# Regrouping a block's small matmuls, naming the PSUM banks they borrow, and moving two sums to GpSimd

## The chip, the core and the metric

One core of a Trainium2 chip runs the whole kernel. The metric is device microseconds (us) of one execution. TensorE multiplies and writes to PSUM, of which this kernel's pools hold eight banks. In this kernel VectorE and ScalarE read PSUM, and GpSimd works from SBUF. Most executions of one kernel here agree within about 1 us of 276, so differences under 0.5% are read from the traces. There the blocks in the middle of the kernel repeat to about 0.02 us, except block 5 of the kernel before: 14.85 us in its own trace, 14.75 and 14.77 in two runs that leave that block's code alone (light, tail).

## The reference, cut to what matters

```python
def reference(q, k, v, w_in, w_out, beta):        # 8 batches, 8 heads, 576 tokens, 64 per head
    # attention inside chunks of 64 tokens
    scores = (q_c @ k_c.T) / 8
    attn = softmax(scores)
    x = (attn @ v_c).transpose(0, 2, 1, 3).reshape(4608, 512)
    # feed-forward, d_ff = 2048
    h = x @ w_in
    g = h * sigmoid(beta * h)
    return g @ w_out
```

## The kernel before

It works through nine blocks, 0 to 8, of 512 tokens. From block 2 on, each block has a first GEMM (x @ w_in, then Silu on ScalarE) and a second (g @ w_out). The second, and one half of the first, save a product by sums and differences of quarters (seven products in place of eight). Beside them run the attention of the next block (PV: probabilities times v) and the scores of the one after that. PV works on 64x64 tiles of TensorE, the scores on 32x64 tiles, the GEMMs on the whole array.

The second GEMM is seven products of 16 matmuls, `mm[0]` to `mm[6]`, on banks A, B, A, D, A, C, A. A collects three sums in turn, which ScalarE copies out on the way (u1, u2, u3). Before the change banks come from a ring of four:

```python
ps_p = ctx.enter_context(tc.tile_pool(name="ps_p", bufs=4, space=bass.MemoryType.PSUM))
def grab(name):
    bank[name] = ps_p.tile([128, 2, HM], FP32, tag="p", name=f"o{name}")
def mm2():
    prod("A", s_(3), t3, False)
    take("u2", "A")                       # ScalarE copies A
    ...
    nc.gpsimd.tensor_tensor(out=sb["w1"], in0=sb["u1"], in1=sb["u2"], op=ALU.subtract)
def cB():                                 # VectorE adds u1 straight from bank B
    store(j, 0, 0, comb("B", sb["u1"]))
```

This is the order within a block, with lines joined and block 1's own calls left out (`late` is block 1, `light` are blocks 6 to 8, of which 8 has no PV left; `dve(n)` issues n waiting sums of quarters on VectorE; each `pvs` is two PVs and their normalisation):

```python
mm[0]()
if not late and not light: dve(2)
emit_sum(j, 3, 1); emit_sum(j, 3, 3)
...
pvs(0)
mm[1]()
if light: dve(2); pvs(2)
dve(6)
mm[2]()
if not late and not light: pvs(2)
if na + 1 < NB and not late: table(ACTF.Exp)
mm[3]()
for p in (0, 2, 1, 3): emit_sum(j, 4, p)  # s4, which mm[5] needs
cB()
mm[4]()
cD()
if na + 1 < NB:
    emit_sc(2 * na + 2, "x")              # 128 small matmuls in one run
    emit_sc(2 * na + 3)
T(j + 3); emit_xs(na)
mm[5](); cC(); mm[6]()
```

The softmax here doesn't subtract the row's maximum and nothing guards it: scores larger than these inputs give would overflow.

Of the kernel before, what the change touches and what calls it, by code (L numbers as in the profile page):

```python
# [8 lines left out]
FP32 = mybir.dt.float32  # L9
FP16 = mybir.dt.float16  # L10
# [5 lines left out]
def kernel(  # L16
# [10 lines left out]
    nc = tc.nc  # L27
# [27 lines left out]
    xs_p = ctx.enter_context(tc.tile_pool(name="xs", bufs=1))  # L55
    c_p = ctx.enter_context(tc.tile_pool(name="c", bufs=2))
    osb_p = ctx.enter_context(tc.tile_pool(name="osb", bufs=4))
    ps_p = ctx.enter_context(tc.tile_pool(name="ps_p", bufs=4, space=bass.MemoryType.PSUM))
    ps_s = ctx.enter_context(tc.tile_pool(name="ps_s", bufs=1, space=bass.MemoryType.PSUM))
    ps_x = ctx.enter_context(tc.tile_pool(name="ps_x", bufs=1, space=bass.MemoryType.PSUM))  # L60

    ident = const.tile([128, 128], FP16)
    bstage = const.tile([128, 2, 32], FP32)
# [84 lines left out]
    def sc_part(g, z, sc):  # L148
        for c in range(4):
            b, cb = divmod(4 * g + c, NCB)  # L150
            for e in range(2):
                for a in range(4):
# [8 lines left out]
                        stop=(e == 1),  # L161
                    )

    def emit_sc(g, where="s"):
        if where == "x":
            scx = ps_x.tile([128, 2, 2, 4, CH], FP32, tag="x", name="scx")
            sc = [scx[:, 0], scx[:, 1]]
        else:
            sc = [
                ps_p.tile([128, 2, 4, CH], FP32, tag="p", name=f"scp{s}") if where == "p"  # L170
                else ps_s.tile([128, 2, 4, CH], FP32, tag=f"sc{s}", name=f"sc{s}")
                for s in range(2)
            ]
        for z in range(2):
            sc_part(g, z, sc)
        et = et_t[g] = et_p.tile([128, 2, 2, 4, CH], FP16, tag="et", name="et")
        for o, i_ in [(et, scx)] if where == "x" else [(et[:, s], sc[s]) for s in range(2)]:
            nc.scalar.activation(out=o, in_=i_, func=ACTF.Exp, scale=scale)
# [16 lines left out]
        return x16.rearrange("p e s d -> p (e s d)")  # L195

    def emit_pv(i, where="x", xbar=True):
        g = i // 2
        spare = where != "x"
        if where == "p":  # L200
            xs = [ps_p.tile([128, 4, 128], FP32, tag="p", name="xp") for _ in range(2)]
        elif where == "s":
            xs = [ps_s.tile([128, 4, 128], FP32, tag=f"sc{h}", name="xp") for h in range(2)]
        else:
            x = ps_x.tile([128, 2, 4, 128], FP32, tag="x", name="x")
            xs = [x[:, 0], x[:, 1]]
        for s in range(4):
            z, a2 = s // 2, s % 2
            for hp, cp in ((0, 0), (1, 1), (0, 1), (1, 0)):
                b, cb = divmod(2 * i + cp, NCB)  # L210
                p0, o0 = 64 * hp, 64 * cp
                nc.tensor.matmul(  # L212
                    out=xs[hp][o0:o0 + 64, s, 0:D + 1],
                    lhsT=et_t[g][p0:p0 + 64, a2, z, 2 * (i % 2) + cp, :],
                    rhs=vbuf[b % NV][p0:p0 + 64, s, cb, 0:D + 1],
                )
        xf = normed(xs, None if spare else x)
        j, t0 = i // 4, (i % 4) * 128
        if j not in xt_t:
            xt_t[j] = xt_p.tile([128, KDM, BLK], FP16, tag="xt", name="xt")  # L220
        if xbar:
            nc.sync.dma_start_transpose(out=xt_t[j][:, :, t0:t0 + 128], in_=xf)
        else:
            x16_t[i] = xf

    def emit_xp(i, where="s", eng=None):
        xf = x16_t.pop(i)
        j, t0 = i // 4, (i % 4) * 128
        pool, tag = {"s": (ps_s, f"sc{i % 2}"), "p": (ps_p, "p"), "x": (ps_x, "x")}[where]
        xps = pool.tile([128, KDM, 128], FP16, tag=tag, name="xps")  # L230
        for kk in range(KDM):
            nc.tensor.transpose(
                out=xps[:, kk, :], in_=xf[:, kk * 128:(kk + 1) * 128], identity=ident
            )
        if eng:
            eng.tensor_copy(out=xt_t[j][:, :, t0:t0 + 128], in_=xps)
        else:
            nc.scalar.copy(out=xt_t[j][:, :, t0:t0 + 128], in_=xps)

    def emit_idle(n, w=512, d=None):  # L240
        if d is None:
            d = ps_p.tile([128, BLK], FP32, tag="p", name="idle")
        for _ in range(n):
            nc.tensor.matmul(
                out=d[:, 0:w], lhsT=zero[:, 0:128], rhs=zero[:, 0:w], start=True, stop=True)
        return d
# [6 lines left out]

    def emit_h(j, m, c0=0, c1=BLK, ns=range(KDM)):
        if (j, m) not in hps_t:
            hps_t[j, m] = ps_p.tile([128, BLK], FP32, tag="p", name="hps")
        for n in ns:
            e, z = n // 2, n % 2
            nc.tensor.matmul(  # L259
                out=hps_t[j, m][:, c0:c1],  # L260
                lhsT=w_r[m // 4][:, 2 * z + e, m // 2 % 2, m % 2, :],
                rhs=xt_t[j][:, n, c0:c1],
                start=(n == 0 and c0 == 0),
                stop=(n == KDM - 1),
                skip_group_check=True,
            )
# [132 lines left out]
    def steps_L2(j, last=False):  # L399
# [5 lines left out]
        bank = {}  # L405
        sb = {}

        def grab(name):
            bank[name] = ps_p.tile([128, 2, HM], FP32, tag="p", name=f"o{name}")

        def prod(name, a, b, first, order=KO):
            if first and name not in bank:
# [25 lines left out]
        s_ = lambda n: s_t[j][n - 1]  # L438

        def mm0():  # L440
            grab("B")
            prod("A", g[:, 0:NM, up], b11, True, order=(0, 1, 4, 5, 6, 7, 2, 3))
            take("u1", "A")

# [10 lines left out]

        def mm3():
            prod("D", g[:, NM:KFF, dn], t4, True)
            if last:
                take("d", "D")

        def mm4():
            if last:
# [16 lines left out]
        def mm6():  # L479
# [7 lines left out]
                store(j, 0, 1, o2)  # L487
                return
            for i in range(2):
                pc = ps_p.tile([128, HM], FP32, tag="p", name="oCi")  # L490
                for kk in range(NM):
                    nc.tensor.matmul(
                        out=pc, lhsT=s_(4)[:, kk, i * 128:(i + 1) * 128], rhs=b22[:, kk, :],
                        start=(kk == 0), stop=(kk == NM - 1),
                    )
                o = osb_p.tile([128, HM], FP32, tag=f"oe{i}", bufs=1, name=f"oe{i}")
                nc.vector.tensor_tensor(out=o, in0=pc, in1=sb["t"][:, i], op=ALU.add)
                r0 = j * BLK + i * 128
                (nc.sync, nc.scalar)[i].dma_start(out=out[r0:r0 + 128, HM:DM], in_=o)

        def cB():
            store(j, 0, 0, comb("B", sb["u1"]))

        def cD():
            store(j, 1, 0, comb("A", sb["d"]) if last else comb("D", sb["u3"]))
            if last:
                nc.vector.tensor_tensor(out=sb["w1"], in0=bank["A"], in1=sb["w1"], op=ALU.add)

        def cC():
            comb("C", sb["w1"], keep="t")  # L510

        return [mm0, mm1, mm2, mm3, mm4, mm5, mm6], cB, cD, cC

    def L2_plain(j):
        ops = [ps_p.tile([128, DM], FP32, tag="p", name="ops") for _ in range(4)]

        def part(kk, t):
            nc.tensor.matmul(  # L518
# [30 lines left out]
    def head_sc(z):  # L549
        if z == 0:  # L550
            for g in range(2):
                sc_h[g] = [
                    ps_s.tile([128, 2, 4, CH], FP32, tag=f"sc{s}", name=f"sc{s}") if g == 0
                    else ps_p.tile([128, 2, 4, CH], FP32, tag="p", name=f"scp{s}")
                    for s in range(2)
                ]
                et_t[g] = et_p.tile([128, 2, 2, 4, CH], FP16, tag="et", name="et")
# [24 lines left out]
    def head_xp(g, z, where, eng=None):  # L582
        xf = x16_t.pop((g, z))
        if 0 not in xt_t:
            xt_t[0] = xt_p.tile([128, KDM, BLK], FP16, tag="xt", name="xt")
        pool, tag = {"x": (ps_x, "x"), "s1": (ps_s, "sc1"), "p": (ps_p, "p")}[where]
        xps = pool.tile([128, KDM, 128], FP16, tag=tag, name="xps")
        for kk in range(KDM):
            nc.tensor.transpose(
                out=xps[:, kk, :], in_=xf[:, kk * 128:(kk + 1) * 128], identity=ident  # L590
# [66 lines left out]
    with tc.manual_schedule():  # L657
# [93 lines left out]
        for j in range(1, NB):  # L751
# [16 lines left out]
                if na < NB:  # L768
                    emit_pv(4 * na + n, where)

            mm, cB, cD, cC = steps_L2(j, last=(j == NB - 1))
            def pvs(n):
                pv(n, "x")
                pv(n + 1, "s")

            light = j + 2 >= B
            mm[0]()
            if not late and not light:
                dve(2)
# [2 lines left out]
            if late:  # L782
                dve(8)
                T(3, 2)
            else:
                pvs(0)
            mm[1]()
            if late:
                pvs(0)
            if light:  # L790
                dve(2)
                pvs(2)
            dve(6)
            mm[2]()
            if not late and not light:
                pvs(2)
            if na + 1 < NB and not late:
                table(ACTF.Exp)
            mm[3]()
            if late:  # L800
                pvs(2)
            for p in (0, 2, 1, 3):
                emit_sum(j, 4, p)
            cB()
            mm[4]()
            cD()
            if na + 1 < NB:
                emit_sc(2 * na + 2, "x")
                emit_sc(2 * na + 3)
            T(j + 3)  # L810
            if na < NB:
                emit_xs(na)
            mm[5]()
            if j < NB - 1:
                cC()
            mm[6]()
            if na + 1 < NB:
                table(ACTF.Silu)


# [28 lines left out]
```

## Time and profile before

| | before |
|---|---|
| time | 276.43 us (3 runs, 275.59 to 277.12) |
| TensorE, VectorE, ScalarE, GpSimd busy | 97, 78, 60, 35% of the span |
| second GEMM of blocks 2, 3, 4, 5, 6, 7 | 14.63, 14.61, 14.65, 14.85, 14.73, 13.43 us |
| from the last matmul's start to the end | 3.73 us |

The second GEMM's length is the distance, in TensorE's timeline, from the start of the first product on A to the start of the next block's first product. It includes everything small that is issued in between. The prediction shows TensorE's side for block 5. ScalarE's timeline of block 5 before (start, length, group; the bracket is idle time and who ended it), two of its lines, shows the Silus that free the last banks, and the idle time in front of the u2 copy:

```profile
178.50 1.24 ACT L270 ACTIVATE gt<-hps,beta 128x512 f16<-128x512 f32 x2
183.02 0.59 ACT L427 COPY u<-oA 128x512 f32<-128x512 f32 x1 [2.81 <-PE oA L416]
```

VectorE's timeline of the same block has the four s4 sums that the product at C needs, done 1 us before that product starts at 188.43:

```profile
186.01 1.42 DVE L380 TENSOR_TENSOR s<-gt,s 128x512 f16<-128x512 f16 x4
```

### The profile page before, as it was taken

To read this page: it belongs to the slowest core of one execution; us is meant where nothing else is said; L and a number is where in the kernel's file an instruction comes from. 1 tells how busy PE (TensorE), PEld (TensorE's weight loads), DVE (VectorE), ACT (ScalarE), POOL (GpSimd) and SP (SyncE) were. 2 spreads that over 40 slices of the span, in tenths; PEclk is the share of its full clock that TensorE was granted. 3 is DMA by queue.
4 is the path that set the end of the run, shared out by engine and by line. 5 is a ranking of instruction groups with operands and counts; after the bars stand their busy time and mean duration, and the time that the engine had idled before them with its cause. 6 is when DMAs were issued, how large, how long until landed. Compare 5 with 4: busy or idle time off the path is not lost.

```text
span 275.0 us, 8686 instructions
## 1 busy us (share of the span) xinstructions
PE 266.9 (97%) x3751; PEld 197.1 (72%) x3751; DVE 214.9 (78%) x429; ACT 164.3 (60%) x281; POOL 96.8 (35%) x107
## 2 busy tenths in 40 slices
PE   8699999999999999999999999999999999999994
PEld 5379544857886688768876886688668866886784
DVE  2673674877888999799989988997689768986844
ACT  2169527879166845784578447854784478316820
POOL 8643446171108720772077205720311031112110
PEclk9999999999999999999999999999999999999999
DMA  6999999999967934893479242924202320232013
GB/s 103 171 200 210 210 181 208 194 261 199 90 135 144 172 44 117 173 163 42 117 158 173 45 120 76 87 42 117 79 0 60 100 76 0 55 104 76 0 42 114
DMA packets 69654, 32.02 MB, mean 116 GB/s; under 512 B 53744, under 2 KB 63984, under 8 KB 69616
## 3 DMA queue, kind: packets, MB, share of 16 engines
q0 software_dynamic: 45024, 18.35, 55.3%
q1 hardware_dynamic: 24448, 12.99, 18.1%
q8 instruction: 29, 0.48, 0.7%
q10 hardware_dynamic: 144, 0.13, 0.1%
q14 instruction: 9, 0.07, 0.1%
HBM read 36.71 MB, written 9.44 MB: 168 GB/s over the span
## 4 chain that ended last, share of the span: by engine, by line
PE 79%; DMA 14%; DVE 3%; issue 1%; ACT 1%; POOL 1%; DVEq 0%; ACTq 0%; POOLq 0%
PE hps L259 22%; PE oA L416 19%; PE wA L313 9%; PE wX L313 7%; DMA w_out<-in_moe_w_out_dram 6%; PE oB L416 5%; PE oD L416 5%; DMA wi<-in_moe_w_in_dram 4%; PE oC L416 4%; DMA ku<-in_k_dram 3%; PE ops L518 2%; PE x L212 2%; DMA xt<-x 1%; PE scx L156 1%; PE sc L156 1%
## 5 line engine op out<-in xcount | busy, mean ns | idle before, releaser
L259 PE MATMUL hps<-xt,wi 128*128 128x512 f16 (+2 forms) x528 | 85.2, 308 | 0.2
L270 ACT ACTIVATE gt<-hps,beta 128x512 f16<-128x512 f32 x88 | 57.8, 683 | 20.9 <-PE hps L259 20.7
L259 PEld LDWEIGHTS <-wi 128*128 128x128 f16 x528 | 42.8, 98 | 23.2 <-DMA wi<-in_moe_w_in_dram 0.2
L416 PEld LDWEIGHTS <-s 128*128 128x128 f16 x496 | 47.6, 98 | 6.2 <-DVE s L376 0.5
L416 PE MATMUL oA<-tw,s 128*128 128x256 f16 x368 | 44.2, 273 | 0.0
L416 PEld LDWEIGHTS <-gt 128*128 128x128 f16 x384 | 36.3, 98 | 6.6
L427 ACT COPY u<-oA 128x512 f32<-128x512 f32 x24 | 14.0, 585 | 40.3 <-PE oA L416 40.3
L321 DVE COPY u<-wA 128x512 f32<-128x512 f32 x42 | 28.6, 682 | 4.5 <-PE wA L313 4.5
L99 POOL DMA_DIRECT2D vb<-in_v_dram x32 | 27.4, 873 | 6.3 <-DMA w_out<-in_moe_w_out_dram 3.3
L344 POOL TENSOR_TENSOR t<-u,w 128x512 f32<-128x512 f32 x14 | 17.8, 1274 | 33.5 <-DVE u L321 33.5
L313 PEld LDWEIGHTS <-sw 128*128 128x128 f16 x224 | 21.9, 98 | 9.2 <-issue 0.7
L486 POOL TENSOR_TENSOR o<-t,o 128x512 f32<-128x512 f32 x7 | 8.9, 1271 | 51.7 <-ACT o L483 42.9
L454 POOL TENSOR_TENSOR w<-u,u 128x512 f32<-128x512 f32 x7 | 9.8, 1407 | 47.2 <-ACT u L427 25.9
L135 DVE STREAM_TRANSPOSE qT<-qu 128x576 f32<-128x576 f32 x16 | 20.0, 1252 | 6.4 <-DMA qu<-in_q_dram 6.2
L135 DVE STREAM_TRANSPOSE kT<-ku 128x576 f32<-128x576 f32 x16 | 19.9, 1244 | 3.6 <-DMA ku<-in_k_dram 3.5
L313 PEld LDWEIGHTS <-wi 128*128 128x128 f16 x168 | 16.4, 98 | 4.9
L655 ACT ACT_TABLE_LOAD x15 | 19.2, 1283 | 0.3
L324 ACT ACTIVATE gt<-c,beta 128x512 f16<-128x512 f32 x28 | 18.7, 716 | 0.3
L374 DVE TENSOR_TENSOR s<-gt 128x512 f16<-128x512 f16 x32 | 17.8, 555 | 0.0
L313 PE MATMUL wA<-xs,sw 128*128 128x256 f16 x112 | 16.8, 273 | 0.5 <-DVE u L321 0.5
L376 DVE TENSOR_TENSOR s<-s,gt 128x512 f16<-128x512 f16 x32 | 15.6, 488 | 1.1
L518 PE MATMUL ops<-w_out,gt 128*128 128x512 f16 x64 | 15.1, 379 | 0.4 <-ACT w_out L122 0.2
(96 smaller groups left out, 404.6 us busy)
## 6 DMA issues: line engine op xcount, KB each, us to landing
out_dram<-osb SPq DMA_DIRECT2D x21, 256.0 KB, 3.1
vb<-in_v_dram POOLq DMA_DIRECT2D x32, 144.0 KB, 8.1
out_dram<-o SPq DMA_DIRECT2D x14, 256.0 KB, 2.2
qu<-in_q_dram POOLq DMA_DIRECT2D x6, 576.0 KB, 7.8
ku<-in_k_dram POOLq DMA_DIRECT2D x6, 576.0 KB, 10.0
wi<-in_moe_w_in_dram POOLq DMA_DIRECT2D x3, 512.0 KB, 11.5
w_out<-in_moe_w_out_dram POOLq DMA_DIRECT2D x3, 512.0 KB, 15.5
qu<-in_q_dram POOLq DMA_DIRECT2D x4, 288.0 KB, 12.0
```

The lines of the kernel that those rows point to most:

```text
L99: nc.gpsimd.dma_start(out=t[64 * hp:64 * hp + 64, 2 * z:2 * z + 2, :, 0:D].rearrange("p s c d -> p (s c) d"), in_=v[b, h0:h0 + 2].rearrang ...
L135: nc.vector.transpose(out=dst[b][:, z].rearrange("p t r e -> p (t r e)").bitcast(FP32).rearrange("p (t r) -> p r t", r=RUN), in_=src[b][:, ...
L259: nc.tensor.matmul(out=hps_t[j, m][:, c0:c1], lhsT=w_r[m // 4][:, 2 * z + e, m // 2 % 2, m % 2, :], rhs=xt_t[j][:, n, c0:c1], start=(n == ...
L270: nc.scalar.activation(out=gt_t[j][:, m, :], in_=hps, func=ACTF.Silu, scale=beta2[:, m % 2, m // 2:m // 2 + 1],)
L313: nc.tensor.matmul(out=bank[b][:, i, :], lhsT=a[:, kk, q, i, :], rhs=rhs[:, kk, :], start=(first and i == 0 and kk == 0), stop=(kk == 1), ...
L321: nc.vector.tensor_copy(out=sb[nm], in_=bank[b])
L324: nc.scalar.activation(out=gt_t[j][:, m, cols], in_=src, func=ACTF.Silu, scale=beta2[:, m % 2, m // 2:m // 2 + 1],)
L344: nc.gpsimd.tensor_tensor(out=sb["t"], in0=sb["u3"], in1=sb["w1"], op=ALU.add)
L374: tt(out=s1[:, lo], in0=g[:, lo, dn], in1=g[:, hi, dn], op=ALU.add)
L416: nc.tensor.matmul(out=bank[name][:, i, :], lhsT=a[:, kk, i * 128:(i + 1) * 128], rhs=b[:, kk, :], start=(first and i == 0 and n == 0), st ...
L518: nc.tensor.matmul(out=ops[t], lhsT=gt_t[j][:, kk, t * 128:(t + 1) * 128], rhs=wo(kk), start=(kk == 0), stop=(kk == KFF - 1),)
L655: nc.scalar.activation(out=warm2, in_=warm, func=func, scale=1.0)
```

## The change

Its intent is to have two excursions into small matmuls per block, not three, each of a PV pair and half of the scores. For that, scores must be written to banks that the GEMM uses too, in the middle of it. So the banks get names, the banks' order is chosen for blocks 2 to 6, and B is copied out by ScalarE at once; its sum is made later by GpSimd. In the last block one sum moves to GpSimd and one ScalarE copy goes. The core of the diff, with some lines joined:

```diff
-    ps_p = ... tile_pool(name="ps_p", bufs=4, space=bass.MemoryType.PSUM)
+    ps_p = ... tile_pool(name="ps_p", bufs=1, space=bass.MemoryType.PSUM)
+    rot = [0, 1, 2, 3]
+    def pt(shape, dt, name, slot=None):            # a bank by its number, or the oldest
...
+        o = (0, 3, 1, 2) if 1 < j < NB - 2 else (0, 1, 2, 3)
+        slot = {n: r[i] for n, i in zip("ABDC", o)}
...
+        def cB0():
+            nc.scalar.copy(out=sb["o11"], in_=bank["B"])
+        def cB1():
+            nc.gpsimd.tensor_tensor(out=sb["o11"], in0=sb["o11"], in1=sb["u1"], op=ALU.add)
+            store(j, 0, 0, sb["o11"])
         def cD():
-            store(j, 1, 0, comb("A", sb["d"]) if last else comb("D", sb["u3"]))
             if last:
-                nc.vector.tensor_tensor(out=sb["w1"], in0=bank["A"], in1=sb["w1"], op=ALU.add)
+                nc.gpsimd.tensor_tensor(out=sb["w1"], in0=sb["u3"], in1=sb["w1"], op=ALU.add)
+            store(j, 1, 0, comb("D", sb["u3"]))
...                                                  # blocks 2 to 7
-                pvs(0)
-            mm[1]()
...
+                attn(0, [slot["D"], slot["C"]])     # PV, PV, half of the scores, exp
+                mm[1]()
+                if ahead:
+                    cB0()
+                dve(8)
+                mm[2]()
+                attn(2, [slot["B"], slot["C"]])
+                mm[3]()
             for p in (0, 2, 1, 3):
                 emit_sum(j, 4, p)
-            cB()
+            (cB() if late or not ahead else cB1())
             mm[4]()
+            if not late: T(j + 3)
             cD()
-            if na + 1 < NB:
-                emit_sc(2 * na + 2, "x")
-                emit_sc(2 * na + 3)
```

## The prediction

> **What bounds the kernel now.** I read the page's busy table first, then TensorE's waits, then the chain that ended last, then TensorE's timeline of one block of 512 tokens.
>
> ```profile
> PE 266.9 (97%) x3751; PEld 197.1 (72%) x3751; DVE 214.9 (78%) x429; ACT 164.3 (60%) x281; POOL 96.8 (35%) x107
> ```
>
> TensorE is busy for 97% of the span, but the legend warns that matmuls are pipelined and a busy PE is not one at its peak. So the question is what it waits for. The waits view of TensorE answers with five lines in all:
>
> ```profile
> PE sc L156 <- DVE bt L689: 1.9, 1, 1.9
> PE idle L244 <- DVE zero L659: 1.2, 1, 1.2
> PE wA L313 <- DVE u L321: 0.5, 1, 0.5
> PE sc L156 <- DVE kT L135: 0.4, 1, 0.4
> PE ops L518 <- ACT w_out L122: 0.2, 1, 0.2
> ```
>
> All of it lies in the first 83 us; between 95 us and 270 us the same view is empty. From there on the order of TensorE's own instructions sets the time, and only shorter issue can shorten the span. What is lost there must be read from distances between starts. This is TensorE's timeline in the second GEMM of block 5 (start, length, group):
>
> ```profile
> 177.08 1.93 PE L416 MATMUL oA<-w_out,gt 128*128 128x256 f16 x16
> 178.94 0.32 PE L212 MATMUL x<-vb,et 64*64 64x65 f16 x16
> 179.09 0.30 PE L212 MATMUL xp<-vb,et 64*64 64x65 f16 x16
> 179.32 1.92 PE L416 MATMUL oB<-w_out,gt 128*128 128x256 f16 x16
> 181.07 1.91 PE L416 MATMUL oA<-tw,s 128*128 128x256 f16 x16
> 182.91 0.32 PE L212 MATMUL x<-vb,et 64*64 64x65 f16 x16
> 183.06 0.49 PE L212 MATMUL xp<-vb,et 64*64 64x65 f16 x16
> 183.49 1.92 PE L416 MATMUL oD<-tw,gt 128*128 128x256 f16 x16
> 185.25 1.91 PE L416 MATMUL oA<-tw,s 128*128 128x256 f16 x16
> 187.09 0.71 PE L156 MATMUL scx<-qT,kT 32*64 32x64 f16 x64
> 187.62 0.87 PE L156 MATMUL sc<-qT,kT 32*64 32x64 f16 x64
> 188.43 1.92 PE L416 MATMUL oC<-w_out,s 128*128 128x256 f16 x16
> ```
>
> A product of 16 large matmuls takes 1.75 us from start to start where another large one follows (179.32 to 181.07). Where a small group follows it takes 1.84 to 1.86, so entering costs 0.09 to 0.1. A PV group takes 0.38 us, or 0.58 where it is disturbed (183.06: half a group takes 0.43 in place of 0.23). The scores take 1.34: their first 64 matmuls 0.53, their last 64 0.81. In block 6, the timeline shows those last 64 take 0.67. Sixteen PV matmuls take 0.15 when others of their kind follow and 0.23 when a large one does: 0.08 to leave the small group, and for the scores 0.67 - 0.53 = 0.14. So each excursion into small matmuls costs about 0.09 + 0.08 to 0.14, some 0.2 us, beyond its own streaming, and a block has three: PV, PV, scores. The whole second GEMM with them is 14.85 us (177.08 to 191.93), of which 7 x 1.75 = 12.25 are large; 2.6 us are small work and its edges.
>
> **What the Trainium skill says.** "TensorEngine Tiling (Array Packing)", Tiling Modes (Key Properties), says that changing the tiling mode drains TensorE, changing only the tile doesn't. The edges of about 0.1 us above agree. No run yet shows a change from 64x64 tiles straight to 32x64 ones, which the new order has. "SBUF — State Buffer", Who interferes with whom, says a VectorE operation with two SBUF inputs fully blocks on a GpSimd operation that reads SBUF. The trace agrees: in block 6 GpSimd's u1 - u2 runs from 212.19 for 1.26 us, and the VectorE sum beside it takes 1.43 us where its like takes 0.42:
>
> ```profile
> 211.84 0.42 DVE L374 TENSOR_TENSOR s<-gt 128x512 f16<-128x512 f16 x1
> 212.29 1.43 DVE L376 TENSOR_TENSOR s<-s,gt 128x512 f16<-128x512 f16 x1
> 213.65 1.42 DVE L380 TENSOR_TENSOR s<-gt,s 128x512 f16<-128x512 f16 x4
> ```
>
> "PSUM — Partial Sum Buffer", The four PSUM rules, says GpSimd can't touch PSUM; hence the change's extra ScalarE copy before a GpSimd add. "ScalarE: Activation LUTs", What ACT_TABLE_LOAD costs, gives 1283 ns, as does the trace (15 loads, mean 1283), and a drain of about 1380 more, which the trace doesn't show: after the load at 183.62 the next activation starts at 184.92.
>
> **The change part by part.** It matters in blocks 2 to 6 of 0 to 8; block 1 keeps its order, and block 7 only moves a PV pair.
>
> (1) Three small groups become two, each a PV pair (32 matmuls) then half the scores (64). One entry and one exit go: -0.2 us a block. In their place come two direct changes from 64x64 to 32x64 tiles. By the entries and exits I take 0.1 each, +0.2 a block; this is the number I know least, with 0.03 to 0.15 possible. Net 0.0.
>
> (2) The pause in the last half of the scores (0.81 against 0.67 in block 6). It comes late in 128 matmuls issued some 8 ns apart; a group is now 96 with fewer of the fast kind in a row. I give it two thirds of 0.14 in four blocks: -0.4 us in all.
>
> (3) The disturbed PV groups: block 5 loses 0.2; blocks 6 and 7 have the second PV pair at once after the next product, where it takes 0.48 (209.02 to 209.50 in block 6) in place of 0.38, and they lose 0.13 more where the s2 sum, blocked by GpSimd, comes late for the product at 213.00 (its 16 matmuls last 2.05, not 1.91). Now all pending sums precede the second pair. -0.2 - 2 x (0.1 + 0.13) = -0.65. New multi-bank writes may need extra semaphore instructions of their own: +0.3.
>
> (4) ScalarE gains a copy of B (0.585) and one exp call (4 x 0.6 in place of 1.02 + 2 x 0.6) per block; its two table loads a block only move. It is idle for 2.81 us before 183.02 and 2.07 before 187.19, so this fits. The order holds too: u1 is copied by 180.2, the table and two exps take until about 182.8, the copy of B until 183.4, and the second scores, which want banks B and C, start near 184.1. The first scores want the banks of the 14th and 15th activations, of which the later ends at about 179.1, and start at about 179.3.
>
> (5) VectorE loses the add of B (0.68 a block); GpSimd gains one of 1.27. That one directly follows u1 - u2, so about 184.2 to 186.7, across the start of the s4 sums at 186.0: they lose up to 0.7, then must be there for the product at about 188.1. They end by 188.0, in an order that matches, so nothing is added. VectorE's saving is worth nothing by itself.
>
> (6) The last block: w1 + A on VectorE becomes w1 + u3 on GpSimd, and the copy of D on ScalarE goes. The end waits for the product E (ready near 269.9), two adds from it, and the two final adds; VectorE now starts on E about 0.1 earlier. -0.1.
>
> Sum: 0.0 - 0.4 - 0.65 + 0.3 - 0.1 = about -0.9; with the change of tiles as the trace's clean edges suggest it a little more. I write -1.1: 275.3 us.
>
> **The rivals.** (a) The direct change of tiles is nearly free: then part (1) gives up to 5 x 0.17 = 0.9 more, 274.4. (b) It costs a full exit and entry, 0.2: 5 x 0.2 = 1.0 less, 276.3, the same as before. (c) A new wait: the second scores for the copy of B (0.7 us in hand), the C product for s4 (0.1 to 1), or the next block's first VectorE copies because its tail moved back. Up to 0.5 in each of five blocks, 277.8; for it speaks that VectorE has 24.85 of 27.60 us in block 3, against it that all waits of TensorE on it are hidden now. (d) The big win is impossible: all that the timeline shows beyond streaming after 95 us is some 4 us, under the 5.5 that 2% need.
>
> **Range and chances.** The size is settled by an edge of 0.1 us times ten and a few pauses; runs of the kernel before alone spread over 1.5 us. So 273.6 to 276.9 holds (a), (b) and half of (c). Faster by 2% would need more than there is: 1%. Slower by 2% would need a new wait of 1 us in each block: 2%.
>
> **What would show it.** In TensorE's timeline of a middle block: two small groups, each of about 1.1 us (from the PV's start to the next large product), a distance of 0.2 to 0.3 from the second half of the PV to the scores, and no longer distances than 1.75 between large ones. Block length 27.5 to 27.7 in place of 27.7 to 27.9. TensorE's waits after 95 us still empty. In VectorE's timeline an s4 sum stretched by GpSimd. I am wrong if the change of tiles costs over 0.25, if the pauses return in the new groups, or if ScalarE's order makes the large product at B or D wait.

## The result, and the profile after

| | before | after |
|---|---|---|
| time, median of 6 runs | 276.61 us | 275.28 us (274.62 to 275.79) |
| ratio of fast runs | | 0.9955, 95% interval 0.9931 to 0.998 |
| second GEMM of blocks 2 to 7, us | 14.63, 14.61, 14.65, 14.85, 14.73, 13.43 | 14.53, 14.51, 14.53, 14.61, 14.47, 13.19 |
| last matmul's start to the end | 3.73 us | 3.61 us |
| from block 2's second GEMM to the end | 180.94 us | 179.73 us |

A ratio is the mean time of one kernel's fast runs over that of the other's of the same rounds, so it isn't quite the ratio of the medians. The last row leaves out the start, which ends anywhere between 93.2 and 94.5 us in the traces.

The kernel is 0.45% faster. The middle of the kernel says where: 0.10 to 0.12 us in each of blocks 2 to 4, 0.24 to 0.26 in blocks 5 to 7, 0.12 at the end. Of block 5's 0.24, some 0.1 may be the run: against light and tail, whose block 5 is as before, it is 0.14 to 0.16.

The changed kernel's page (engine, busy us, share of the span, instructions) is nearly the one before:

```profile
PE 265.2 (97%) x3751; PEld 197.1 (72%) x3751; DVE 213.1 (78%) x423; ACT 166.1 (61%) x290; POOL 103.2 (38%) x113
```

Its waits of TensorE add up to 5.3 us, all before 95 us as before; in the window from 95 to 270 us the view is again empty. The longest:

```profile
PE ops L553 <- ACT w_out L130: 1.3, 3, 0.9
```

TensorE's timeline of block 5 after:

```profile
176.84 1.93 PE L445 MATMUL oA<-w_out,gt 128*128 128x256 f16 x16
178.70 0.32 PE L233 MATMUL x<-vb,et 64*64 64x65 f16 x16
178.85 0.30 PE L233 MATMUL xp<-vb,et 64*64 64x65 f16 x16
179.07 0.71 PE L164 MATMUL scp<-qT,kT 32*64 32x64 f16 x64
179.72 1.92 PE L445 MATMUL oB<-w_out,gt 128*128 128x256 f16 x16
181.47 1.91 PE L445 MATMUL oA<-tw,s 128*128 128x256 f16 x16
183.31 0.32 PE L233 MATMUL x<-vb,et 64*64 64x65 f16 x16
183.46 0.42 PE L233 MATMUL xp<-vb,et 64*64 64x65 f16 x16
183.81 0.71 PE L164 MATMUL scp<-qT,kT 32*64 32x64 f16 x64
184.45 1.92 PE L445 MATMUL oD<-tw,gt 128*128 128x256 f16 x16
186.21 1.91 PE L445 MATMUL oA<-tw,s 128*128 128x256 f16 x16
187.96 1.91 PE L445 MATMUL oC<-w_out,s 128*128 128x256 f16 x16
```

Read the starts. A small group is 1.02 us (178.70 to 179.72), or 1.14 where the second PV is disturbed as before (183.46 to 183.81 is 0.35 in place of 0.22). The half of the scores takes 0.64 or 0.65 to the next large product here, and 0.64 to 0.69 in all ten groups of the trace: about what the undisturbed second half took before (0.67 in block 6), and never 0.81. The second half of the PV takes 0.22 up to the scores, as it does up to a large product: the direct change of tiles is not cheap, but no dearer than an exit.

Three lines of ScalarE's timeline of block 5 after show the copy of B (L532) in time: it ends at 182.93, the second scores start at 183.81.

```profile
178.26 1.24 ACT L294 ACTIVATE gt<-hps,beta 128x512 f16<-128x512 f32 x2
181.39 1.06 ACT L175 ACTIVATE et<-scp 128x512 f16<-128x512 f32 x2
182.34 0.59 ACT L532 COPY o<-oB 128x512 f32<-128x512 f32 x1
```

GpSimd's two sums, u1 - u2 and then B + u1:

```profile
184.15 1.27 POOL L482 TENSOR_TENSOR w<-u,u 128x512 f32<-128x512 f32 x1 [5.96 <-ACT u L456]
185.38 1.26 POOL L535 TENSOR_TENSOR o<-o,u 128x512 f32<-128x512 f32 x1
```

They hold up VectorE's s4 sums, which take 2.15 us, not 1.42, and end at 187.92 where the product at C starts at 187.96 and takes them one by one. Here the margin is nearly used up, yet nothing is added:

```profile
185.77 2.15 DVE L404 TENSOR_TENSOR s<-gt,s 128x512 f16<-128x512 f16 x4
```

### The profile page after: what moved, and what is told of

The parts are those of the page before. It is cut to its first block, busy times and chain, and to the rows that moved or that the text cites. A ratio compares the mean times of both kernels' runs of the same rounds, so it can differ in the third digit from the quotient of the medians.

```text
span 273.9 us, 8696 instructions
## 1 busy us (share of the span) xinstructions
PE 265.2 (97%) x3751; PEld 197.1 (72%) x3751; DVE 213.1 (78%) x423; ACT 166.1 (61%) x290; POOL 103.2 (38%) x113
## 4 chain that ended last, share of the span: by engine, by line
PE 78%; DMA 15%; DVE 3%; POOL 2%; issue 1%; ACT 0%; DVEq 0%; POOLq 0%
PE hps L283 22%; PE oA L445 19%; PE wA L337 9%; PE wX L337 7%; DMA qu<-in_q_dram 6%; PE oB L445 5%; PE oD L445 5%; DMA w_out<-in_moe_w_out_dram 4%; PE oC L445 4%; DMA vb<-in_v_dram 3%; PE scp L164 2%; DMA xt<-x 2%; PE x L233 1%; PE ops L553 1%; POOL vb L107 1%
## 5 line engine op out<-in xcount | busy, mean ns | idle before, releaser
L445 PEld LDWEIGHTS <-s 128*128 128x128 f16 x496 | 48.3, 98 | 5.7
L482 POOL TENSOR_TENSOR w<-u,u 128x512 f32<-128x512 f32 x7 | 8.9, 1265 | 49.3 <-ACT u L456 49.3
L509 ACT COPY o<-oA 128x512 f32<-128x512 f32 x7 | 4.1, 585 | 19.7 <-PE oA L445 19.7
```

The source lines that it names most:

```text
L445: nc.tensor.matmul(out=bank[name][:, i, :], lhsT=a[:, kk, i * 128:(i + 1) * 128], rhs=b[:, kk, :], start=(first and i == 0 and n == 0), st ...
```

## The experiments

All twelve ran with correct results. Ratios are to the kernel before in the same rounds. "Rest" is the time in the trace from the start of block 2's second GEMM to the end; "mid" is the second GEMM of blocks 2, 3, 4, 5 and 6.

| run | median, us | ratio to before | mid, us | block 7 | rest, us |
|---|---|---|---|---|---|
| before | 276.61 | | 14.63 14.61 14.65 14.85 14.73 | 13.43 | 180.94 |
| after | 275.28 | 0.9955 | 14.53 14.51 14.53 14.61 14.47 | 13.19 | 179.73 |
| again | 275.85 | 0.9958 | 14.53 14.51 14.53 14.61 14.47 | 13.19 | 179.72 |
| split | 278.68 | 1.0077 | 15.16 15.16 15.15 15.35 14.98 | 13.19 | 182.88 |
| split2 | 276.50 | 0.9988 | 14.70 14.69 14.69 14.89 14.69 | 13.19 | 180.73 |
| mix | 276.66 | 1.0003 | 14.75 14.75 14.75 14.75 14.71 | 13.19 | 180.77 |
| ring | 277.95 | 1.0039 | 14.95 14.95 15.00 15.07 14.78 | 13.19 | 181.84 |
| dveB | 278.05 | 1.0057 | 15.14 15.12 15.09 15.10 14.47 | 13.19 | 182.02 |
| addDVE | 275.54 | 0.9956 | 14.53 14.51 14.53 14.60 14.47 | 13.19 | 179.72 |
| light | 276.42 | 0.9995 | 14.62 14.62 14.64 14.75 14.50 | 13.19 | 180.84 |
| tail | 276.18 (one run) | | 14.64 14.62 14.64 14.77 14.74 | 13.43 | 180.85 |
| three | 276.98 | 1.0038 | 15.03 15.04 15.09 14.77 14.81 | 13.19 | 181.81 |
| longer | 283.54 | 1.0199 | 15.06 16.21 15.07 15.14 19.05 | 13.19 | 187.61 |
| double | 290.70 (three fast runs) | 1.0502 | profile only at a low clock | | |

**again: the changed kernel itself.** No edit.

> The changed kernel once more, unaltered, as the reference of this group of runs: ratio near 0.9955 to the kernel before; second GEMM of blocks 2 to 6 at 14.5 us; any change of TensorE's waits before 95 us is a matter of the run.

Ratio 0.9958 and the same block lengths to 0.01 us. So the mid columns of the new order can be compared at a few hundredths.

**split: is it the grouping?** The scores leave the groups and get their own, one product later.

```diff
-                attn(0, [slot["D"], slot["C"]])
+                attn(0)
                 mm[1]()
+                scores(0, [slot["D"], slot["C"]])
...
-                attn(2, [slot["B"], slot["C"]])
+                attn(2)
                 mm[3]()
+                scores(2, [slot["B"], slot["C"]])
```

> The changed kernel with each half of the scores in a group of its own, one product after its PV pair: four small groups in blocks 2 to 6 in place of two, no direct change from 64x64 to 32x64 tiles. Theory (edges of small groups on TensorE): each of the ten halves swaps a direct change (0.11 us and 0.04 for the slow first four) for an exit and an entry (0.12 + 0.09 + 0.04), so +0.10 each, +1.0 us in all, 276.3 us; the second GEMM of blocks 2 to 6 grows from 14.51 to about 14.7. Rival (the grouping does nothing, the gain came from the work taken off VectorE or from the named banks, which both stay): no change, 275.3 us.

It missed: 0.51 to 0.74 us a block more, not 0.2, by a wait of TensorE that neither theory had. In its waits:

```profile
PE oB L445 <- ACT gt L294: 1.9, 5, 0.4
```

The product at B is now due 2.2 us into the block and starts at 2.7: the chosen order puts B in the bank of the block's last Silu, which ends about 2.66 us into it. In the changed kernel the scores stand in between and B starts at 2.88, 0.2 us after that Silu. The bank order and the grouping belong together.

**split2: the same without that wait.**

```diff
-        o = (0, 3, 1, 2) if 1 < j < NB - 2 else (0, 1, 2, 3)
+        o = (0, 1, 2, 3)
```

> Run split had a confounding wait: with no scores ahead of it, the product at B came at 2.2 us into the block and stood 0.6 us for the last Silu, whose bank B takes in the named order. Here the same split, with B in the bank released earlier (ring order of banks). Theory (edges): ten times exit 0.117 + entry 0.093 + slow start 0.036 less the direct change 0.112 + 0.036 = +0.10 each; second GEMM of blocks 2 to 6 at 14.7, +1.0 us against the changed kernel. Rival (four short groups cost no more than two long ones once that wait is gone): 14.5 and no difference.

Blocks 2 to 4 are 0.16 to 0.18 longer than in the changed kernel, five blocks 1.01 us together, as the theory had it (0.20 each, 1.0 in all). Each half of the scores in a group of its own costs 0.08 to 0.09 us more than beside a PV pair; the ratio of the same round rises from 0.9958 to 0.9988, though the two intervals overlap, so this rests on the traces. Four groups are dearer than two. In block 4 the product at B takes 1.85 us to the scores, where it takes 1.76 to another large one (entry), and the scores take 0.64, as in the group with a PV pair:

```profile
151.30 1.92 PE L445 MATMUL oB<-w_out,gt 128*128 128x256 f16 x16
153.15 0.71 PE L164 MATMUL scp<-qT,kT 32*64 32x64 f16 x64
153.79 1.92 PE L445 MATMUL oA<-tw,s 128*128 128x256 f16 x16
```

Block 5 grew most, by 0.28 us; one of its runs of 64 scores has a pause of 0.08 us. Compared with the changed kernel, this run has the other order of banks too, but TensorE's waits after 95 us are empty in both.

**mix: what does a direct change of tiles cost?** The scores stand between the two PVs of a pair.

```diff
-                ps = [pv_mm(4 * na + n, "x"), pv_mm(4 * na + n + 1, "s")]
+                ps = [pv_mm(4 * na + n, "x")]
                 if ahead and slots:
                     sc = emit_sc_in(g, slots)
+                ps.append(pv_mm(4 * na + n + 1, "s"))
```

> The changed kernel with the scores between the two PVs of a pair, which adds one direct change of tiles (32x64 back to 64x64) to each of the ten groups and nothing else. Theory (a direct change of tiles drains TensorE and costs 0.11 plus 0.03 for the slow first four): +0.145 each, +1.45 us, 276.7 us; second GEMM of blocks 2 to 6 from 14.51 to 14.8. Rival (the distance seen before the scores is the wait for their banks, not the change of tiles): under 0.05 each, so under +0.5 us.

Blocks 2 to 4 grow by 0.22 to 0.24, so 0.115 us for each change, not 0.145; the rival's limit of 0.05 is passed. Its timeline:

```profile
179.67 0.32 PE L233 MATMUL x<-vb,et 64*64 64x65 f16 x16
179.92 0.73 PE L164 MATMUL scp<-qT,kT 32*64 32x64 f16 x64
180.58 0.32 PE L233 MATMUL xp<-vb,et 64*64 64x65 f16 x16
180.83 1.92 PE L445 MATMUL oB<-w_out,gt 128*128 128x256 f16 x16
```

The first 16 PV matmuls take 0.25 to the scores, where they took 0.15 to their own kind. The new step from the scores back to PV waits for no new bank, and costs about as much: the 64 scores take 0.66 up to it, as they do up to a large product, and 0.53 up to more scores.

**ring: what is naming the banks worth?** The edit of split2, on the changed kernel.

> The changed kernel with its banks in ring order (A, B, D, C take the banks in the order of their release) in place of the named order. Theory (the named order is there so that the early scores avoid the bank of the last Silu): that Silu ends about 2.66 us into the block, the scores now want its bank for C at 2.24, so they stand about 0.45 us, second GEMM of blocks 2 to 6 at 14.95, +2.2 us against the changed kernel. Rival (naming is only tidiness): 14.5 us.

0.42 to 0.47 us more in blocks 2 to 5, as expected. In its timeline of TensorE the first score matmul is issued, and the rest stand for the last Silu:

```profile
180.76 0.70 PE L164 MATMUL scp<-qT,kT 32*64 32x64 f16 x63 [0.27 <-ACT gt L294]
```

With the ring's order the regrouping would have gained nothing: the ratio is 1.0039 (0.9998 to 1.0079), and the trace from block 2 on is 0.90 us longer than that of the kernel before.

**dveB: is ScalarE's copy needed?** VectorE adds u1 to B from the bank, at the same place in the order.

```diff
-                    cB0()
+                    cB()
                 dve(8)
...
-                cB1()
```

> The changed kernel with B's sum made by VectorE straight from the bank after its product, in place of ScalarE's copy and GpSimd's add: VectorE gets 0.68 us a block back, GpSimd loses 1.27. Theory (VectorE is off the path, the copy only serves to empty B early): 275.3 us within 0.3, second GEMM of blocks 2 to 6 still 14.5, s4 sums no longer stretched by GpSimd (1.4 us for the four in place of 2.15). Rival (VectorE's relief is what pays): 0.3 to 0.7 us more in each of five blocks, 277 to 278.7 us.

The theory fell, and in the rival's direction: 0.49 to 0.61 us more in blocks 2 to 5 (none in block 6, which has four waiting sums there, not six). The s4 sums are indeed no longer stretched (1.42), but they start later: 0.68 us of work stands ahead of them, and the u1 - u2 of GpSimd now blocks one waiting sum on its way (1.38 us in place of 0.42). TensorE's product at C starts up to 0.25 us late and then waits for them piece by piece: its 16 matmuls last 2.27, not 1.91, and take 2.10 to the next start, not 1.75.

```profile
160.94 2.27 PE L445 MATMUL oC<-w_out,s 128*128 128x256 f16 x16
```

The waits view of TensorE's matmuls is empty after 95 us in this run too, although TensorE stands here. The same view of its weight loads (PEld) has it, four waits in each of four blocks:

```profile
PEld L445 <- DVE s L404: 3.9, 16, 0.4
```

**addDVE: or is it VectorE's load?** ScalarE's copy stays; the add goes to VectorE, after the s4 sums.

```diff
-            nc.gpsimd.tensor_tensor(out=sb["o11"], in0=sb["o11"], in1=sb["u1"], op=ALU.add)
+            nc.vector.tensor_tensor(out=sb["o11"], in0=sb["o11"], in1=sb["u1"], op=ALU.add)
```

> The changed kernel with ScalarE's early copy of B kept, but the add u1 + B on VectorE after the s4 sums, in place of GpSimd. Run dveB lost 0.6 us a block since VectorE did B's work before the s4 sums. Theory (only what stands ahead of the s4 sums counts): no loss, second GEMM of blocks 2 to 6 at 14.5, s4 sums 1.4 us and not 2.15, changed kernel's time within 0.3 us. Rival (VectorE has no 0.68 us to spare anywhere in the block): the next block's first GEMM stretches from 13.02 to 13.2 or more, +0.5 to +1 us.

The same as the changed kernel to 0.01 us in every block, s4 sums at 1.42. So VectorE's 0.68 us matter only ahead of the s4 sums. Of the two ways tried to empty B early, only ScalarE's copy costs nothing; GpSimd's add isn't needed.

**light: blocks 6 and 7 alone.** On the kernel before, the second PV pair of these blocks moves one product later, with all waiting sums ahead of it.

```diff
-            if light:
-                dve(2)
-                pvs(2)
-            dve(6)
+            dve(8 if light else 6)
             mm[2]()
-            if not late and not light:
+            if not late:
                 pvs(2)
```

> The kernel before with one thing of the change: in blocks 6 and 7 all waiting sums go ahead of the second PV pair, and that pair one product later. Theory (the pauses of blocks 6 and 7 came from this pair and from the sum s2 being late): second GEMM of block 6 from 14.73 to about 14.6 and of block 7 from 13.43 to 13.19, as in the changed kernel; -0.35 to -0.5 us, 276.1. Rival (these two blocks gained by the banks or by GpSimd's and ScalarE's part): no change in either block.

Block 6 gains 0.23 and block 7 gains 0.24, all that the change gained in block 7. The time shows none of it (0.9995, interval 0.9973 to 1.0018): in its trace three first GEMMs (blocks 3, 5 and 6) took 13.12 to 13.29 us, not 13.02, since VectorE was late with a copy that TensorE needs; in the longest of the three it had itself waited 1.11 us for a transfer of x. The kernel before has such a case too (13.05), and tail (13.12). In the ten traces of kernels with the new order, first GEMMs from block 3 on take 13.02 without exception. Whether the new order or the run decides that was not tested.

**tail: the last block alone**, on the kernel before.

```diff
-            if last:
-                take("d", "D")
...
-            store(j, 1, 0, comb("A", sb["d"]) if last else comb("D", sb["u3"]))
             if last:
-                nc.vector.tensor_tensor(out=sb["w1"], in0=bank["A"], in1=sb["w1"], op=ALU.add)
+                nc.gpsimd.tensor_tensor(out=sb["w1"], in0=sb["u3"], in1=sb["w1"], op=ALU.add)
+            store(j, 1, 0, comb("D", sb["u3"]))
```

> The kernel before with the last block's differences on GpSimd alone. Theory: VectorE is free when the product E is ready, about 0.1 us sooner, so from the last matmul's start to the end takes 3.6 us in place of 3.73. All else the same. Rival (the end is set by the final products and stores): 3.7 us.

3.64 us from the last matmul to the end, against 3.73; one look, without rounds, so it leans on the trace.

**three: fewer direct changes.** Three PVs in the first group, the fourth and all scores in the second.

```diff
-                attn(0, [slot["D"], slot["C"]])
+                attn3()            # PV 0, 1, 2, the last on banks D and C
                 mm[1]()
...
-                attn(2, [slot["B"], slot["C"]])
+                attn1()            # PV 3, then all 128 scores
```

> The changed kernel regrouped: three PVs without scores in the first group, the fourth PV and all the scores in the second, so one direct change of tiles a block in place of two. Theory: -0.145 a block for the change of tiles, +0.05 to +0.1 for the pause that a run of 144 brings back: -0.05 to -0.1 a block, second GEMM of blocks 2 to 6 near 14.43, 274.9 us. Rival (a new wait: VectorE must empty banks D and C of the third PV, and ScalarE has four exps at once): over 14.6, 275.8 us or more.

A miss of the theory, for split's reason: the first group is too short. B's product starts 0.30 to 0.45 us after the last PV matmul in each of the five blocks, where 0.125 is usual, since it waits for the last Silu. And in four of the five long runs of small matmuls, pauses of 0.09 to 0.16 us are back.

**double and longer: what are the pauses in long runs?** Every half of the scores is computed twice, or its first half is.

```diff
-        for z in range(2):
+        for z in (0, 1, 0, 1):        # double; longer has (0, 0, 1)
             sc_part(g, z, sc)
```

> The changed kernel with every half of the scores computed twice, same banks, same result: a group is 32 + 128 small matmuls. Theory (the pause in the scores of the kernel before comes with the length of an unbroken run of small matmuls, after some 80 to 100): 640 more matmuls at 8.3 ns are 5.3 us, and pauses of about 0.1 come back in most of the ten groups, 6.0 to 6.6 us more, 281.3 to 281.9. Rival (the pause was a wait for the second pair of score banks): 5.3 us more and smooth runs.

> The changed kernel with the first 32 matmuls of each half of the scores done twice: a group is 32 + 96 small matmuls, 128 as long as the scores' run in the kernel before; run double (32 + 128) fell to a clock of 0.657 in its profile and so showed nothing at full clock. Theory (a pause comes after some 80 to 110 small matmuls in one unbroken run): +320 matmuls of 8.3 ns = 2.7 us, and pauses of about 0.1 us in most of the ten groups: 3.2 to 3.7 us, 278.7 us. Rival (the pause belonged to the change of score banks in the kernel before): 2.7 us and no distance over 0.05 us within a run of scores.

double settled nothing. Its profiled run was at a granted clock of 0.657 and took 398.79 us; its three fast runs took 288.27 to 291.42, more than either theory, without a trace. longer has a profile at clock 0.994. Nine of its ten groups, of 32 + 96 small matmuls, are smooth, so length alone, as I had put it, does not bring the pause. The rival, score banks, isn't borne out either, as three has pauses elsewhere in its runs. What the pauses of 0.08 to 0.125 us in the kernel before are stays open; shown is that they come in scores' runs of 128, after the 85th matmul or later, in four of five blocks, and in none of the changed kernel's ten runs of 64. One of 0.08 in a run of 64 in split2 says that short runs aren't safe from them.

The rest of longer's excess is something else. Twice TensorE stood with no releaser; these are two of its waits:

```profile
PE oD L445 <- issue: 2.3, 1, 2.3
PE scp L164 <- issue: 1.0, 1, 1.0
```

In the trace's list of instructions the two stops are exactly 12 times 256 TensorE instructions apart, and the instruction queue reads 16,384 bytes at a time, which is 256 instructions of 64 bytes if TensorE's 7,502 fill its 29 reads in the kernel before. Each stop ends 1.37 to 1.38 us after a read ended (read from 216.22 to 217.18, stop from 216.0 to 218.55). double's trace, slow as it is, has a third: a stop that ends at 299.06, 13 times 256 instructions after the place of longer's first, and 1.48 us after a read. The likely reading is that TensorE had used up its instructions before the next ones were there; it is inferred from these three cases, not tried. After longer's first stop, of 1.0 us, the clock stayed at 1.00. After the second it fell: the view by stretches (stretch, then busy time with instruction counts by engine, granted clock, DMA share, GB/s) has it at 0.52:

```profile
218.50:222.00 3.50, 3.44 (x17) 2.48 (x18) 0.61 (x2) 0.00 (x0) 0.00 (x0) 0.52 0.44 117
```

## Why the prediction was right

275.3 us was predicted, 275.28 measured; nearer than the method deserves, as the sum was 0.9 and I wrote 1.1, and the start alone moves by 1 us from run to run. The part free of that start lost 1.21 us. Step by step:

- **The bound** was right in the main: TensorE's own order of issue. But the empty waits view after 95 us is weaker evidence than the prediction made it, as dveB shows, and its own part (3) names a wait of 0.13 us that the view lacks. The view of the weight loads of the kernel before has it, once each in blocks 6 and 7, and after the change it is gone:

```profile
PEld L416 <- DVE s L376: 0.5, 2, 0.2
```

- **(1) Edges.** "I take 0.1 each" for the direct change: mix measured 0.115. Entry and exit as 0.2: split2 gives 0.115 + 0.085 = 0.20. So regrouping by itself is worth next to nothing (-0.20 + 2 x 0.115 = +0.03 a block; block 6, which had no pause, gained 0.03 beyond what light gained there), where 0.0 was predicted. That the change from 64x64 to 32x64 costs what mix's added change back does is taken over; in the changed kernel's ten groups the first score starts 0.119 to 0.123 us after the last PV matmul, where matmuls of one kind follow each other in about 0.008, so it is close. Rivals (a), nearly free, and (b), 0.2, are both ruled out.
- **(2) The pause in the scores.** Predicted -0.4 in all. It is gone everywhere: the four pauses of blocks 2 to 5 were 0.41 together, of which the new groups lose 0.02 to 0.05 again in each of blocks 2 to 4. This is most of the -0.10 to -0.12 of these blocks. Why it comes is not settled, so this term was right by the old trace's statistics rather than by an understood cause.
- **(3) Disturbed PV groups.** -0.65 predicted. Blocks 6 and 7 gave 0.26 and 0.24; light shows nearly all of it without the regrouping. For block 5 the prediction took 0.2, and that was wrong: its second PV half went from 0.43 to 0.35, not to 0.23, and it takes 0.35 in light and tail too, so the change didn't cure it. Together that is at most 0.58. The +0.3 for new semaphore instructions was not there: that is the term most mis-sized. With it at zero the sum would have been -1.15. The good total thus owes something to two errors, +0.3 and block 5, that partly cancel.
- **(4) ScalarE** fits as laid out; the copy of B ends 0.9 us before the scores want the bank. I named the Silu's bank for the first scores, but not what hangs on it: in ring, and in split against split2, the last Silu's bank is wanted too early, which costs 0.42 to 0.47 us in each of blocks 2 to 5. So an order of banks that fits the grouping is a condition of the gain.
- **(5) VectorE and GpSimd.** The s4 sums lose 0.73 us to GpSimd ("up to 0.7") and still end in time. "VectorE's saving is worth nothing by itself" holds for its place before the change (addDVE), and is wrong where B must be emptied early: there VectorE's 0.68 us would cost about 0.6 a block (dveB). Rival (c), a new wait, was thus real in two forms, but the change avoids both.
- **(6) The end** gave 0.12, or 0.09 alone (tail), for 0.1.

None of the variants beat the changed kernel; addDVE equals it.

## What to carry to other kernels

When TensorE hardly waits, read the distances between starts, and ask for its weight loads' waits as well as its matmuls'. An excursion into small tiles had a price of its own here (0.2 us), and merging two kinds of small work saved next to nothing, since they use different tiles (0.115 for each change). A bank that is borrowed in the middle is best chosen by when its last user frees it. Whether work on another engine is free depends on what stands behind it in that engine's queue, not on its load.

## What the Trainium skill lacked or had wrong

- "TensorEngine Tiling (Array Packing)", Tiling Modes, says that a change of tiling mode drains TensorE, but gives no cost. Here: 0.115 us from 32x64 to 64x64 (mix), about 0.2 for leaving and entering the full array together (split2 and mix).
- "TensorE: Matmul & The Clock Gate", Why this matters for your kernels, warns of idle gaps over about 3 us. Here a gap of 2.3 us was followed by a granted clock of 0.52 over the next 3.5 us (longer). It is one case.
- "Runtime: NRT & Kernel Launch", Instruction fetch mechanics, says that crossing a 16 KiB boundary is mostly hidden. In longer, with 320 more small matmuls, TensorE stood 1.0 and 2.3 us at what looks like such boundaries; in the kernels before and after it did not.
- No page read has the pauses of 0.08 to 0.125 us late in a run of 128 small matmuls.
- "ScalarE: Activation LUTs", What ACT_TABLE_LOAD costs, adds a drain of about 1.38 us to each load. The trace has the 1.283 us, and no such drain: in the kernel before, ScalarE starts its next activation 0.011 us after each load.
